# Attention with linear features: queries' and keys' projections in own pairs of PSUM banks, one lasting pair for all transposes, and a new order of a step

## The chip, the cores and the metric

The kernel runs on one core of a Trainium2 chip. Time is device microseconds (us) of one execution. Engines: PE is TensorE, which multiplies and transposes and writes to PSUM; DVE (VectorE) and ACT (ScalarE) read PSUM and work elementwise; POOL is GpSimd; SP issues most transfers. PSUM has eight banks; a tile of 2 x 512 float32 per partition is a pair of them. Each engine takes its own instructions in order and waits on semaphores for the others.

## The reference, cut to what matters

```
# 8 batches x 8 heads, 576 positions, head_dim 64, 128 features
def phi(x):
    proj = x @ w_phi
    proj = proj - max(abs(proj), axis=-1)
    return concat([exp(proj), exp(-proj)], axis=-1)
q_p, k_p = phi(q), phi(k)
kv  = sum over positions of k_p (x) v        # per batch and head
z   = sum over positions of k_p
out = (q_p @ kv) / (q_p @ z + 1e-6)
# then  h = x @ w_in;  x = (h * cos(h)) @ w_out     (4608 tokens, 512 -> 2048 -> 512)
# then  8 experts, one per token: gate * relu(x @ w1[e]) @ w2[e]
```

## The kernel before

Attention comes first, the dense layer and the experts follow. Attention works on 16 items; an item is two batches times two heads. Turned, an item has nine blocks of 128 columns (each for two heads' halves); they are cut into five groups, `GR=[(0,2),(2,2),(4,1),(5,2),(7,2)]`: four full ones of two blocks and a half one in the middle. The first item runs in `begin(m)`, the others in `step(j,m)`, m from 0 to 4, one group a step. A step is a software pipeline. For item j and step m it does:

- turn: transposes raw q or k of item j+1 (tile pt) and ACT copies them to qT or kT
- outT: transposes finished rows xs of item j-1, two steps old, to po, and ACT copies them to xo
- proj: PE multiplies qT and kT of group m with w_phi into pj; DVE takes the largest absolute value (m_q, m_k) and subtracts it (t_q, t_k), four instructions
- kexp: ACT makes ke = exp of plus and minus t_k of the group before
- qexp: PE transposes t_q of two groups before (ptt), ACT makes qx = exp of plus and minus it
- kv: PE multiplies ke with v; kvfin copies the sum (kvz) by ACT after groups 2 and 4; in step 0 of an item, kv has 24 matmuls instead of 16, in step 4 it has 8
- num: PE multiplies qx of item j-1 with kvz into pn; DVE makes rd, its reciprocal and xs, which I call the trio

The order on an engine is that of the code, since each instruction is put through `keep`. Among these instructions lie those of the dense layer's weights, one piece a step: ACT's d_t and w, DVE's L457 to L460 (two, one, one, none, in turn).

PSUM in the steps: pj one pair, tr one pair (shared in turn by pt and ptt), po one pair, kv and pn one bank each. In pj the queries lie in columns 0 to 255 of both banks and the keys in 256 to 511. Tiles on one bank are guarded as a whole: an engine that wants a bank waits for the other engines' accesses to it.

Of the kernel before, what the change touches and what calls it, by code (L numbers as in the profile page):

```python
# [45 lines left out]
def attention(tc, ctx, S, ident, q, k, v, w_phi, xt):  # L46
# [73 lines left out]

    T={}
    H=64
    def to(tag,name):

        if not pairs: return ps.tile([P,512],F32,tag=dict(tr="tr",po="nm")[tag],name=name)
        return pairs[0].tile([P,2,512],F32,tag=tag,name=name)
    def over(dst,c,src):

        if not pairs: keep(nc.tensor.transpose(dst[:,c*P:(c+1)*P],src,ident)); return
        for r in range(2): keep(nc.tensor.transpose(dst[:,r,c*H:(c+1)*H],src[r*H:(r+1)*H],ident[r*H:(r+1)*H,r*H:(r+1)*H]))  # L130
    def got(dst,a,c):
        return dst[:,a*P:c*P] if not pairs else dst[:,:,a*H:c*H].rearrange("p r (c t) -> p c r t",t=H)
    def like(x): return x if not pairs else x.rearrange("p (c r t) -> p c r t",r=2,t=H)
    def turn(i,m,tag="tr"):
        pt=to(tag,f"pt_{i}_{m}")
        c=0; made=[]
        for t,c0,n in TURN[m]:
            if (t,i) not in T: T[t,i]=S("xT",f"{t}T_{i}")
            a=c
            for b in range(c0,c0+n):  # L140
                over(pt,c,block(raws[t,i],b)); c+=1
            made.append((like(T[t,i][:,c0*P:(c0+n)*P]),got(pt,a,c)))
        def vec():
            for x,p in made: keep(nc.scalar.copy(x,p))
        return vec

    ts={}
    pj=pp.tile([P,2,512],F32,name="pj")
    def proj(i,g):
        c0,n=GR[g]  # L150
        vecs=[]
        other=i==0 and g in (1,4)
        out=[ps.tile([P,512],F32,tag="nm",name=f"pj_{i}_{g}_{s}") for s in range(2)] if other else [pj[:,s,:] for s in range(2)]
        for t,o in (("q",0),("k",256)):
            x=T[t,i]
            for c in range(n):
                for s in range(2):
                    keep(nc.tensor.matmul(out[s][:,o+c*F:o+(c+1)*F],x[s*D:(s+1)*D,(c0+c)*P:(c0+c+1)*P],w2[s*D:(s+1)*D,:],start=True,stop=True))  # L158
            tt=ts[t,i,g]=S(t+"t",f"t_{t}_{i}_{g}")
            def vec(t=t,o=o,tt=tt):  # L160
                gg=pj[:,:,o:o+n*F].rearrange("p s (c f) -> p s c f",f=F)
                m=ap.tile([P,4],F32,tag=t+"m",name=f"m_{t}_{i}_{g}")[:,:2*n].rearrange("p (s c) -> p s c",s=2)
                keep(nc.vector.tensor_reduce(m,gg,AX.X,ALU.max,apply_absolute_value=True))  # L163
                keep(nc.vector.tensor_tensor(tt[:,:n*256].rearrange("p (s c f) -> p s c f",s=2,f=F),gg,  # L164
                    m.unsqueeze(3).to_broadcast([P,2,n,F]),ALU.subtract))
            vecs.append(vec)
        def by_bank():
            ms=[]
            for s in range(2):
                ms.append(ap.tile([P,4],F32,tag="qk"[s]+"m",name=f"m_{s}_{i}_{g}"))  # L170
                nc.vector.tensor_reduce(ms[s],out[s].rearrange("p (c f) -> p c f",f=F),AX.X,ALU.max,apply_absolute_value=True)
            for o,t in ((0,"q"),(1,"k")):
                for s in range(2):
                    nc.vector.tensor_tensor(ts[t,i,g][:,s*256:(s+1)*256].rearrange("p (c f) -> p c f",f=F),out[s][:,o*256:(o+1)*256].rearrange("p (c f) -> p c f",f=F),
                        ms[s][:,2*o:2*o+2].unsqueeze(2).to_broadcast([P,2,F]),ALU.subtract)
        return [by_bank] if other else vecs
# [37 lines left out]
    def qexp(i,g):  # L214

        n=GR[g][1]; tt=ts.pop(("q",i,g))
        pt=to("tr",f"ptt_{i}_{g}")
        for c in range(n):
            for s in range(2): over(pt,2*c+s,tt[:,(s*n+c)*F:(s*n+c+1)*F])
        w=n*P  # L220
        x=ap.tile([P,1024],F32,tag="qx",name=f"qx_{i}_{g}",bufs=4)
        qx[i,g]=x[:,:4*w].rearrange("p (k h c) -> p k h c",h=2,k=2)
        made=[(like(x[:,kk*2*w:(kk+1)*2*w]),got(pt,0,2*n)) for kk in range(2)]
        def vec():
            for (o,p),sign in zip(made,(1.0,-1.0)): keep(nc.scalar.activation(o,p,AF.Exp,scale=sign))
        return vec

    xss={}; xos={}
    def num(i,g):
# [18 lines left out]
        return vec  # L248

    def outT(i,g):  # L250

        t0,n=GR[g]
        if g==0: xos[i]=ap.tile([P,9*P],F32,tag="xo",name=f"xo_{i}")
        xo=xos[i]; xs=xss.pop((i,g))
        po=to("po",f"po_{i}_{g}")
        for t in range(n): over(po,t,xs[:,t*P:(t+1)*P])
        def vec():
            keep(nc.scalar.copy(like(xo[:,t0*P:(t0+n)*P]),got(po,0,n)))
            if g==4:
# [4 lines left out]
    FIRST=((),((0,1),),((0,2),(0,4)),((1,0),(1,1)),((1,2),(1,3)))
    def at(j,m): return divmod(5*j+m,5)
# [4 lines left out]
        if m==2: ld("v",j+1)  # L270
    def begin(m):

        vecs=[turn(i,n) for i,n in FIRST[m]]
        if m>1: vecs+=[lambda: kexp(0,m-2),qexp(0,m-2)]
        for f in vecs: f()
        loads(0,m)
        yield
# [4 lines left out]
        if m==4: kvfin(0,0)
        yield
    def step(j,m):

# [20 lines left out]
        yield
# [812 lines left out]
```

## Time and profile before

| | |
|---|---|
| three runs | 1597.93, 1592.8, 1597.95 us, median 1597.93 |
| the profiled execution | 1593.69 us, its span 1592.0 us |
| PE busy | 1551.5 us, 97% of the span |
| DVE busy | 1116.7 us, 70% |
| ACT busy | 879.0 us, 55% |
| POOL busy | 398.3 us, 25% |

The shares are means over stages of different kinds. Attention's matmuls run up to 344 us, where the dense layer's have begun; the experts' begin at 1132 us. A matmul's end in the records is modelled, so starts are compared with starts. Records of PE count two for each float32 matmul of projections, kv and pn, and one for each transpose.

### The profile page before, as it was taken

How to read it: one execution, taken by the hardware profiler on the slowest of the kernel's cores; microseconds unless marked ns; L12 is line 12 of the kernel's file. 1: busy time of each engine (PE TensorE's matmuls, PEld its weight loads, DVE VectorE, ACT ScalarE, POOL GpSimd, SP SyncE). 2: the span in 40 equal slices, each digit the busy share in tenths (PEclk: the TensorE clock that was granted, in tenths of full speed). 3: DMA queues.
4: the chain of work that ended last, by engine and by line, in shares of the span. 5: the costliest groups of instructions: out<-in, count | busy, mean ns of one | idle time of the engine just before them, and what ended most of it. 6: DMA issues, size and time to landing. Idle time of an engine off the chain costs nothing.

```text
span 1592.0 us, 35511 instructions
## 1 busy us (share of the span) xinstructions
PE 1551.5 (97%) x14065; PEld 1338.9 (84%) x14065; DVE 1116.7 (70%) x2305; ACT 879.0 (55%) x1627; POOL 398.3 (25%) x356
## 2 busy tenths in 40 slices
PE   8899998989999999999999999999999999999998
PEld 7788888878888888888888888888898899899986
DVE  6998988978666767675766667655775656666646
ACT  6777777766534444343534344444765656565646
POOL 1101101120233333243333433333212112212212
PEclk9999999999999999999999999999999999999999
DMA  7755555313200101010100001004749667766752
GB/s 213 213 157 161 153 156 161 105 65 125 92 29 9 40 14 40 7 41 14 40 14 30 24 7 41 7 1 159 237 154 319 224 221 276 239 222 220 246 196 86
DMA packets 140851, 189.33 MB, mean 119 GB/s; under 512 B 63015, under 2 KB 87719, under 8 KB 140674
## 3 DMA queue, kind: packets, MB, share of 16 engines
q1 hardware_dynamic: 132754, 166.11, 33.4%
q0 software_dynamic: 7760, 20.79, 3.9%
q8 instruction: 112, 1.84, 0.5%
q14 instruction: 65, 0.53, 0.1%
q10 hardware_dynamic: 160, 0.07, 0.0%
HBM read 155.88 MB, written 31.82 MB: 118 GB/s over the span
## 4 chain that ended last, share of the span: by engine, by line
PE 81%; DVE 11%; DMA 3%; ACT 2%; issue 2%; POOL 0%; POOLq 0%; DVEq 0%; SPq 0%; ACTq 0%
PE ph L514 24%; PE acc L554 19%; PE mh L822 12%; PE po L834 12%; PE acc L559 5%; DMA out_dram<-o,mrec 3%; PE pj L158 3%; DVE t_k L164 2%; DVE t_q L164 2%; DVE m_q L163 2%; DVE m_k L163 2%; PE kv L204 2%; PE pn L240 2%; PE px L804 1%; DVE xs L247 1%
## 5 line engine op out<-in xcount | busy, mean ns | idle before, releaser
L514 PE MATMUL ph<-x,w 128*128 128x512 f32 x1728 | 418.3, 391 | 1.9 <-DVE fr L536 1.9
L514 PEld LDWEIGHTS ph<-x,w 128*128 128x128 f32 x1728 | 322.6, 188 | 70.0 <-DVE fr L536 2.5
L543 POOL TENSOR_TENSOR gl<-fr,gh 128x512 fp32r<-128x512 f32 x130 | 195.5, 1506 | 432.8 <-DVE gh L542 387.3
L777 DVE TENSOR_TENSOR m<-raw,m 128x512 fp32r<-128x512 f32 x320 | 208.3, 688 | 100.7 <-ACT m L776 72.7
L554 PE MATMUL acc<-w,gh 128*128 128x512 f32 x896 | 275.8, 389 | 0.0
L527 ACT ACTIVATE n<-ph 128x512 int32<-128x512 f32 x144 | 86.0, 597 | 271.3 <-PE ph L514 270.8
L776 ACT CAST m<-raw 128x512 fp32r<-128x512 f32 x320 | 188.0, 619 | 39.2 <-PE mh L822 31.0
L822 PE MATMUL mh<-xT,m 128*128 128x256 f32 x1728 | 201.1, 277 | 0.0
L822 PEld LDWEIGHTS mh<-xT,m 128*128 128x128 f32 x1728 | 197.8, 188 | 1.1 <-DVE hl L825 0.8
L529 DVE SCALAR_TENSOR_TENSOR fr<-ph,n 128x512 f32<-128x512 f32 x144 | 99.2, 689 | 140.5 <-ACT n L527 125.6
L554 PEld LDWEIGHTS acc<-w,gh 128*128 128x128 f32 x896 | 168.2, 188 | 35.0
L590 DVE SCALAR_TENSOR_TENSOR junk<-x1T,wg 128x512 f32<-128x512 f32 x224 | 181.0, 808 | 0.0
L834 PE MATMUL po<-m,hh 128*128 128x512 f32 x576 | 179.6, 393 | 0.0
L554 PE MATMUL acc<-w,gl 128*128 128x512 f32 x448 | 174.3, 389 | 0.0
L532 ACT ACTIVATE fr<-fr 128x512 f32<-128x512 f32 x144 | 91.1, 632 | 117.9 <-DVE fr L529 117.8
L536 DVE SCALAR_TENSOR_TENSOR fr<-fr,ph 128x512 f32<-128x512 f32 x144 | 98.8, 686 | 78.2 <-ACT fr L534 78.1
L834 PEld LDWEIGHTS po<-m,hh 128*128 128x128 f32 x576 | 105.2, 188 | 19.7
L834 PE MATMUL po<-m,hl 128*128 128x512 f32 x288 | 112.4, 390 | 0.0
L883 POOL DMA_INDIRECT out_dram<-o,mrec x38 | 42.7, 1124 | 265.5 <-ACT o L882 251.3
L554 PEld LDWEIGHTS acc<-w,gl 128*128 128x128 f32 x448 | 84.1, 188 | 17.5
L534 ACT ACTIVATE fr<-fr 128x512 f32<-128x512 f32 x143 | 90.4, 632 | 4.3
L240 PE MATMUL pn<-kvz,qx 128*64 128x65 f32 x2304 | 86.9, 226 | 3.0 <-DVE xs L247 1.7
(228 smaller groups left out, 2256.6 us busy)
## 6 DMA issues: line engine op xcount, KB each, us to landing
raw<-in_moe_w_dram SPq DMA_DIRECT2D x160, 512.0 KB
xt<-xo SPq DMA_DIRECT2D x16, 576.0 KB
xr<-xt SPq DMA_DIRECT2D x36, 256.0 KB
raw_q<-in_q_dram SPq DMA_DIRECT2D x32, 256.0 KB
raw_k<-in_k_dram SPq DMA_DIRECT2D x32, 256.0 KB
st<-in_moe_w_in_dram SPq DMA_DIRECT2D x16, 512.0 KB
st<-in_moe_w_out_dram SPq DMA_DIRECT2D x16, 512.0 KB
v<-in_v_dram SPq DMA_DIRECT2D x62, 128.0 KB
```

What stands on the lines that cost most here:

```text
L240: keep(nc.tensor.matmul(o[64*c:64*c+64],x[:,sg,h,t*P+64*c:t*P+64*c+64],kvs[i,bb][:,2*h+sg,:],start=sg==0,stop=sg==1,skip_group_check=True))
L514: nc.tensor.matmul(ph,A[:,ws],xhl[u,d][k],start=n[0]==0,stop=n[0]==11); n[0]+=1
L529: ins=nc.vector.scalar_tensor_tensor(g,ph,INV2PI,n,op0=ALU.mult,op1=ALU.subtract)
L532: nc.scalar.activation(g,g,AF.Sin,scale=math.pi)
L536: out0[0]=nc.vector.scalar_tensor_tensor(g,g,-0.5,ph,op0=ALU.add,op1=ALU.mult)
L543: nc.gpsimd.tensor_tensor(gl,g,f32(gh),ALU.subtract)
L554: nc.tensor.matmul(accs[u][c],A[:,ws],B,start=(f==0 and k==0),stop=(f==NF-1 and k==2))
L590: return lambda: tc.keep_in_program_order(nc.vector.scalar_tensor_tensor(junk,x1T[u,c],1.0,wg[e],op0=ALU.mult,op1=ALU.mult,accum_out=lgs[u ...
L776: keep(nc.scalar.copy(h,a))
L777: keep(nc.vector.tensor_tensor(l,a,f32(h),ALU.subtract))
L822: nc.tensor.matmul(ph[:,f2*T:(f2+1)*T],A[:,ws],B[d//2][:,xs],start=n==0,stop=n==11); n+=1
L834: nc.tensor.matmul(po[c],A[:,ws],B,start=(f==0 and j==0),stop=(f==NF2-1 and j==2))
```

## The change

The queries' projection keeps pj; the keys' gets a pair of its own, pjk. There is one pair tr from the first instruction to the end of attention for all transposes of raw data (columns of chunks 0 to 3) and of t_q (chunks 4 to 7); in the first item its two banks are used in turn as whole banks. po has no tile any more: the turned outputs are written into pjk, beside the keys (from chunk 4 on). In the first item the groups alternate between pj and pjk. The order within a step is new. The number of instructions of each kind is the same.

```diff
     pk=ctx.enter_context(tc.tile_pool(name="a_kv",bufs=1,space=PSUM,side="right"))
-    first=ExitStack()
-    ps=first.enter_context(tc.tile_pool(name="a_first",bufs=2,space=PSUM,side="right"))
-    pairs=[]
+    pj,pjk=(pp.tile([P,2,512],F32,tag=n,name=n) for n in ("pj","pjk"))
+    tr=pk.tile([P,2,512],F32,tag="tr",name="tr")
+    flat=itertools.count()
...
-    def to(tag,name):
-
-        if not pairs: return ps.tile([P,512],F32,tag=dict(tr="tr",po="nm")[tag],name=name)
...
-    def got(dst,a,c):
-        return dst[:,a*P:c*P] if not pairs else dst[:,:,a*H:c*H].rearrange("p r (c t) -> p c r t",t=H)
...
+    def whole(srcs):
+
+        pt=tr[:,next(flat)%2,:]
+        for c,x in enumerate(srcs): keep(nc.tensor.transpose(pt[:,c*P:(c+1)*P],x,ident))
+        return pt
+    def turn(i,m,pt=None,base=0):
...
+        if pt is None:
+            pt=whole(srcs)
+            def vec():
+                for x,a,b in made: keep(nc.scalar.copy(x,pt[:,a*P:b*P]))
+        else:
+            for c,x in enumerate(srcs): over(pt,base+c,x)
+            def vec():
+                for x,a,b in made: keep(nc.scalar.copy(like(x),got(pt,base+a,base+b)))
+        return vec
...
+    def proj(i,g,t,out,o=0):
+        c0,n=GR[g]
+        x=T[t,i]
...
+                keep(nc.tensor.matmul(out[:,s,o+c*F:o+(c+1)*F],x[s*D:(s+1)*D,(c0+c)*P:(c0+c+1)*P],w2[s*D:(s+1)*D,:],start=True,stop=True))
+        tt=ts[t,i,g]=S(t+"t",f"t_{t}_{i}_{g}")
         def vec():
-            for x,p in made: keep(nc.scalar.copy(x,p))
+            gg=out[:,:,o:o+n*F].rearrange("p s (c f) -> p s c f",f=F)
+            m=ap.tile([P,4],F32,tag=t+"m",name=f"m_{t}_{i}_{g}")[:,:2*n].rearrange("p (s c) -> p s c",s=2)
+            keep(nc.vector.tensor_reduce(m,gg,AX.X,ALU.max,apply_absolute_value=True))
+            keep(nc.vector.tensor_tensor(tt[:,:n*256].rearrange("p (s c f) -> p s c f",s=2,f=F),gg,
+                m.unsqueeze(3).to_broadcast([P,2,n,F]),ALU.subtract))
...
-    pj=pp.tile([P,2,512],F32,name="pj")
-    def proj(i,g):
...
-        vecs=[]
-        other=i==0 and g in (1,4)
-        out=[ps.tile([P,512],F32,tag="nm",name=f"pj_{i}_{g}_{s}") for s in range(2)] if other else [pj[:,s,:] for s in range(2)]
-        for t,o in (("q",0),("k",256)):
...
     def qexp(i,g):
 
         n=GR[g][1]; tt=ts.pop(("q",i,g))
-        pt=to("tr",f"ptt_{i}_{g}")
...
-        w=n*P
+        srcs=[tt[:,(s*n+c)*F:(s*n+c+1)*F] for c in range(n) for s in range(2)]
...
+        if i==0 and g<3:
+            pt=whole(srcs)
+            made=[(x[:,kk*w:(kk+1)*w],pt[:,:w]) for kk in range(2)]
+        else:
+            for c,y in enumerate(srcs): over(tr,4+c,y)
+            made=[(like(x[:,kk*w:(kk+1)*w]),got(tr,4,4+2*n)) for kk in range(2)]
...
-        po=to("po",f"po_{i}_{g}")
-        for t in range(n): over(po,t,xs[:,t*P:(t+1)*P])
+        po,base=(pjk,4) if (i,g)<(NI-1,0) else (tr,2*(g%2))
+        for t in range(n): over(po,base+t,xs[:,t*P:(t+1)*P])
         def vec():
-            keep(nc.scalar.copy(like(xo[:,t0*P:(t0+n)*P]),got(po,0,n)))
+            keep(nc.scalar.copy(like(xo[:,t0*P:(t0+n)*P]),got(po,base,base+n)))
...
-        vecs=proj(0,m)
+        if m==4: vecs=[proj(0,m,"q",pj),proj(0,m,"k",pjk)]
+        else:
+            out=(pj,pjk)[m%2]
+            vecs=[proj(0,m,"q",out),proj(0,m,"k",out,256)]
+            if m==1: vecs=[lambda: by_bank(0,m,out)]
...
     def step(j,m):
 
-        vecs=[]
-        if j==1 and m==0: vecs=[turn(1,4),turn(2,0,"po")]
-        elif j+1<NI: vecs=[turn(j+1,m)]
-        i,g=at(j-1,m-2)
-        if i>=0: vecs.append(outT(i,g))
-        for f in vecs: f()
-        if (j,m)==(1,0): kexp(0,3)
-        i,g=at(j,m-1)
-        if i<NI: kexp(i,g)
+        vecs=[]; dve=[]
+        i,g=at(j,m-2); oi,og=at(j-1,m-2); ki,kg=at(j,m-1)
+        if j<NI: dve.append(proj(j,m,"q",pj))
+        if oi>=0: vecs.append(outT(oi,og))
+        if j<NI: dve.append(proj(j,m,"k",pjk))
+        two=j==1 and m==0
+        if two: vecs+=[lambda: kexp(0,3),turn(2,0,pjk,4)]
+        if i<NI: last=qexp(i,g)
+        if two: vecs.append(turn(1,4,tr))
+        elif j+1<NI: vecs.append(turn(j+1,m,tr))
+        if i<NI: vecs.append(last)
+        for f in vecs+dve: f()
         loads(j,m)
-        vecs=proj(j,m) if j<NI else []
-        i,g=at(j,m-2)
-        if i<NI: qexp(i,g)()
         yield
-        vecs.append(num(j-1,m))
         if i<NI: kv(i,g)
-        for f in vecs: f()
+        last=num(j-1,m)
         if i<NI and g in (2,4): kvfin(i,g//4)
+        if ki<NI: kexp(ki,kg)
+        last()
...
-    first.close()
-    pairs.append(ctx.enter_context(tc.tile_pool(name="a_pairs",bufs=1,space=PSUM,side="right")))
```

PE, the instructions of one whole step (item 3, step 3); raw_q and qT are the raw and turned queries, xs the finished rows. Before:

```order
L130 MATMUL pt_3_1649<-ident,raw_q_1015 128x64 x8
L130 MATMUL po_1_1658<-ident,xs_1_1531 128x64 x4
L158 MATMUL pj<-w_90,qT_1098 128x128 x4
L158 MATMUL pj<-w_90,kT_883 128x128 x4
L130 MATMUL ptt_1_1678<-ident,t_q_1_1496 128x64 x8
L240 MATMUL pn_3_1690<-kvz_1_1558,qx_3_1400 64x65 x16
L204 MATMUL kv_0_1620<-v_1113,ke_1_1579 64x65 x16
```

The same step in the change:

```order
L156 MATMUL pj<-w_90,qT_1072 128x128 x4
L125 MATMUL pjk<-ident,xs_1_1492 128x64 x4
L156 MATMUL pjk<-w_90,kT_868 128x128 x4
L125 MATMUL tr<-ident,t_q_1_1409 128x64 x8
L125 MATMUL tr<-ident,raw_q_997 128x64 x8
L201 MATMUL kv_0_1552<-v_1088,ke_1_1579 64x65 x16
L240 MATMUL pn_3_1645<-kvz_1_1493,qx_3_1323 64x65 x16
```

The projections moved to the front with the outputs' transposes between them, the raw transposes went behind those of t_q, and pn went from before kv to the end.

DVE, one step (item 4, step 0), with the engines whose semaphores it waits on. Before:

```order
L163 TENSOR_REDUCE m_q_0_1897<-pj 128x4 [waits PE_49]
L164 TENSOR_TENSOR t_q_0_1836<-pj,m_q_0_1897 128x512 [waits DVE_49]
L163 TENSOR_REDUCE m_k_0_1900<-pj 128x4
L164 TENSOR_TENSOR t_k_0_1841<-pj,m_k_0_1900 128x512 [waits DVE_49,Activation_49]
L245 TENSOR_SCALAR rd_0_1903<-pn_0_1854 128x4 [waits PE_49]
```

In the change:

```order
L161 TENSOR_REDUCE m_q_0_1781<-pj 128x4 [waits PE_49]
L162 TENSOR_TENSOR t_q_0_1749<-pj,m_q_0_1781 128x512 [waits DVE_49]
L161 TENSOR_REDUCE m_k_0_1784<-pjk 128x4 [waits Activation_49]
L162 TENSOR_TENSOR t_k_0_1758<-pjk,m_k_0_1784 128x512 [waits DVE_49]
L245 TENSOR_SCALAR rd_0_1833<-pn_0_1812 128x4 [waits PE_49]
```

The order is the same; m_k waits for ACT now, whose copy xo reads the same pair.

ACT, around the end of item 4's last step and the next step's beginning. Before:

```order
L211 COPY kvz_0_2257<-kv_0_2069 128x260
L461 CAST w_0_1810<-d_t_0_1809 128x512
L144 COPY kT_2264<-pt_0_2263 128x512
L258 COPY xo_2019<-po_3_2273 128x256
L184 ACTIVATE ke_4_2280<-t_k_4_2212 128x4x128 x2
L225 ACTIVATE qx_3_2302<-ptt_3_2293 128x512 x2
```

In the change:

```order
L208 COPY kvz_0_2168<-kv_0_1986 128x260
L181 ACTIVATE ke_3_2170<-t_k_3_2034 128x4x128 x2
L464 CAST w_0_1743<-d_t_0_1742 128x512
L258 COPY xo_1943<-pjk 128x256
L147 COPY kT_2204<-tr 128x512
L225 ACTIVATE qx_3_2195<-tr 128x512 x2
```

The copy xo stands first in a step, and the two instructions of ke moved from the middle of a step to its end.

## Rows read from the trace of the kernel before

**Rows 1.** Windows: stretch, its length, each engine's busy us, granted clock, DMA share, GB/s.
```profile
20.00:40.00 20.00, 17.41 (x416) 16.37 (x414) 15.11 (x34) 14.09 (x31) 0.54 (x3) 0.91 0.75 193
80.00:120.00 40.00, 36.33 (x924) 33.73 (x924) 36.21 (x82) 30.29 (x70) 3.68 (x9) 1.00 0.54 156
600.00:1100.00 500.00, 500.00 (x2291) 412.43 (x2290) 334.32 (x749) 206.53 (x327) 184.00 (x129) 1.00 0.11 32
```

**Rows 2.** Chain of waits, 200 to 300 us, its shares by line.
```profile
by line: PE pj L158 15.9%; DVE t_q L164 11.6%; DVE m_q L163 11.2%; DVE t_k L164 11.1%; DVE m_k L163 9.6%; PE kv L204 8.0%; PE pn L240 7.4%; DVE xs L247 3.7%; issue 3.7%; PE pt L130 2.8%; PE ptt L130 1.9%; DVE d_t L460 1.8%; DVE d_t L458 1.7
```

**Rows 3.** Waits of PE, 80 to 320 us: total us, times, longest.
```profile
PE pj L158 <- DVE t_k L164: 12.5, 29, 0.7
PE ptt L130 <- ACT qT L144: 4.3, 4, 1.2
```

**Rows 4.** Waits of DVE, 80 to 320 us: the same columns.
```profile
DVE m_q L163 <- PE pj L158: 11.2, 19, 0.7
```

**Rows 5.** Lines of DVE, 80 to 320 us: count | busy us, mean ns | idle before.
```profile
L163 DVE TENSOR_REDUCE m_q<-pj 128x4 f32<-128x512 f32 (+1 forms) x61 | 38.9, 638 | 12.2 <-PE pj L158 11.2
...
L460 DVE SCALAR_TENSOR_TENSOR d_t<-st,d_t 128x512 int32<-128x512 int32 x16 | 10.9, 682 | 0.0
```

**Rows 6.** Timeline of PE: start, duration, line, output<-inputs, matmuls, idle before and releaser.
```profile
228.61 1.57 PE L204 MATMUL kv<-v,ke 128*64 128x65 f32 x48
230.11 0.46 PE L130 MATMUL pt<-ident,raw_k 64*128 64x64 f32 x8
230.41 0.29 PE L130 MATMUL po<-ident,xs 64*128 64x64 f32 x4
230.53 0.66 PE L158 MATMUL pj<-w,qT 64*128 64x128 f32 x8
231.03 0.61 PE L158 MATMUL pj<-w,kT 64*128 64x128 f32 x8
231.48 0.41 PE L130 MATMUL ptt<-ident,t_q 64*128 64x64 f32 x8
231.82 1.16 PE L240 MATMUL pn<-kvz,qx 128*64 128x65 f32 x32
232.80 1.10 PE L204 MATMUL kv<-v,ke 128*64 128x65 f32 x32
233.84 0.28 PE L130 MATMUL pt<-ident,rl_k 64*128 64x64 f32 x2
...
250.49 0.46 PE L130 MATMUL pt<-ident,raw_k 64*128 64x64 f32 x8
```

**Rows 7.** Timeline of DVE, 250 to 255 us.
```profile
250.60 0.15 DVE L245 TENSOR_SCALAR rd<-pn 128x4 f32<-128x4 f32 x1
...
251.34 0.68 DVE L460 SCALAR_TENSOR_TENSOR d_t<-st,d_t 128x512 int32<-128x512 int32 x1
252.08 0.69 DVE L163 TENSOR_REDUCE m_q<-pj 128x4 f32<-128x512 f32 x1
...
253.41 0.68 DVE L163 TENSOR_REDUCE m_k<-pj 128x4 f32<-128x512 f32 x1
...
254.80 0.15 DVE L245 TENSOR_SCALAR rd<-pn 128x4 f32<-128x4 f32 x1
```

**Rows 8.** Timeline of ACT, 250 to 255 us.
```profile
251.00 0.59 ACT L144 COPY kT<-pt 128x512 f32<-128x512 f32 x1 [1.16 <-PE pt L130]
251.48 0.38 ACT L258 COPY xo<-po 128x256 f32<-128x256 f32 x1
251.74 1.16 ACT L184 ACTIVATE ke<-t_k 128x512 f32<-128x512 f32 x2
252.79 1.08 ACT L225 ACTIVATE qx<-ptt 128x512 f32<-128x512 f32 x2
```

**Rows 9.** Timeline, all engines, around the second item's first step.
```profile
22.96 0.46 PE L130 MATMUL pt<-ident,raw_q 64*128 64x64 f32 x8 [2.29 <-DVE t_k L174]
...
25.00 2.00 PE L240 MATMUL pn<-kvz,qx 128*64 128x65 f32 x32
```

More of the change, by code (lines that the diff above doesn't have):

```diff
@@ L122, in attention @@
     H=64
-    def to(tag,name):
-        if not pairs: return ps.tile([P,512],F32,tag=dict(tr="tr",po="nm")[tag],name=name)
-        return pairs[0].tile([P,2,512],F32,tag=tag,name=name)
     def over(dst,c,src):
-        if not pairs: keep(nc.tensor.transpose(dst[:,c*P:(c+1)*P],src,ident)); return
         for r in range(2): keep(nc.tensor.transpose(dst[:,r,c*H:(c+1)*H],src[r*H:(r+1)*H],ident[r*H:(r+1)*H,r*H:(r+1)*H]))
-    def got(dst,a,c):
-        return dst[:,a*P:c*P] if not pairs else dst[:,:,a*H:c*H].rearrange("p r (c t) -> p c r t",t=H)
@@ L133, in like, with got @@
[L133 to L136, printed above, removed]
+    def got(dst,a,c): return dst[:,:,a*H:c*H].rearrange("p r (c t) -> p c r t",t=H)
+    def like(x): return x.rearrange("p (c r t) -> p c r t",r=2,t=H)
+    def whole(srcs):
[3 more added lines that the diff above has]
+    def turn(i,m,pt=None,base=0):
+        c=0; made=[]; srcs=[]
@@ L137, in turn @@
         for t,c0,n in TURN[m]:
             if (t,i) not in T: T[t,i]=S("xT",f"{t}T_{i}")
[L139 to L143, printed above, removed]
-            for x,p in made: keep(nc.scalar.copy(x,p))
+            srcs+=[block(raws[t,i],b) for b in range(c0,c0+n)]
+            made.append((T[t,i][:,c0*P:(c0+n)*P],c,c+n)); c+=n
+        if pt is None:
[6 more added lines that the diff above has]
+                for x,a,b in made: keep(nc.scalar.copy(like(x),got(pt,base+a,base+b)))
@@ L145, in turn @@
         return vec
     ts={}
-    pj=pp.tile([P,2,512],F32,name="pj")
-    def proj(i,g):
+    def proj(i,g,t,out,o=0):
         c0,n=GR[g]
-        vecs=[]
-        other=i==0 and g in (1,4)
-        out=[ps.tile([P,512],F32,tag="nm",name=f"pj_{i}_{g}_{s}") for s in range(2)] if other else [pj[:,s,:] for s in range(2)]
-        for t,o in (("q",0),("k",256)):
[L155 to L168, printed above, removed]
-            for s in range(2):
[L170 to L176, printed above, removed]
@@ new lines, in proj, with vec @@
+        x=T[t,i]
+        for c in range(n):
+            for s in range(2):
+                keep(nc.tensor.matmul(out[:,s,o+c*F:o+(c+1)*F],x[s*D:(s+1)*D,(c0+c)*P:(c0+c+1)*P],w2[s*D:(s+1)*D,:],start=True,stop=True))
+        tt=ts[t,i,g]=S(t+"t",f"t_{t}_{i}_{g}")
+        def vec():
+            gg=out[:,:,o:o+n*F].rearrange("p s (c f) -> p s c f",f=F)
[3 more added lines that the diff above has]
+                m.unsqueeze(3).to_broadcast([P,2,n,F]),ALU.subtract))
@@ new lines, in proj, with by_bank @@
+        return vec
+    def by_bank(i,g,out):
+        ms=[]
+        for s in range(2):
+            ms.append(ap.tile([P,4],F32,tag="qk"[s]+"m",name=f"m_{s}_{i}_{g}"))
+            keep(nc.vector.tensor_reduce(ms[s],out[:,s,:].rearrange("p (c f) -> p c f",f=F),AX.X,ALU.max,apply_absolute_value=True))
+        for o,t in ((0,"q"),(1,"k")):
+            for s in range(2):
+                keep(nc.vector.tensor_tensor(ts[t,i,g][:,s*256:(s+1)*256].rearrange("p (c f) -> p c f",f=F),out[:,s,o*256:(o+1)*256].rearrange("p (c f) -> p c f",f=F),
+                    ms[s][:,2*o:2*o+2].unsqueeze(2).to_broadcast([P,2,F]),ALU.subtract))
@@ L216, in qexp @@
         n=GR[g][1]; tt=ts.pop(("q",i,g))
-        pt=to("tr",f"ptt_{i}_{g}")
-        for c in range(n):
-            for s in range(2): over(pt,2*c+s,tt[:,(s*n+c)*F:(s*n+c+1)*F])
-        w=n*P
+        srcs=[tt[:,(s*n+c)*F:(s*n+c+1)*F] for c in range(n) for s in range(2)]
+        w=2*n*P
         x=ap.tile([P,1024],F32,tag="qx",name=f"qx_{i}_{g}",bufs=4)
-        qx[i,g]=x[:,:4*w].rearrange("p (k h c) -> p k h c",h=2,k=2)
-        made=[(like(x[:,kk*2*w:(kk+1)*2*w]),got(pt,0,2*n)) for kk in range(2)]
+        qx[i,g]=x[:,:2*w].rearrange("p (k h c) -> p k h c",h=2,k=2)
+        if i==0 and g<3:
[4 more added lines that the diff above has]
+            made=[(like(x[:,kk*w:(kk+1)*w]),got(tr,4,4+2*n)) for kk in range(2)]
         def vec():
@@ L271, in begin @@
     def begin(m):
-        vecs=[turn(i,n) for i,n in FIRST[m]]
-        if m>1: vecs+=[lambda: kexp(0,m-2),qexp(0,m-2)]
-        for f in vecs: f()
+        for i,n in FIRST[m]: turn(i,n)()
+        if m>1:
+            kexp(0,m-2); qexp(0,m-2)()
         loads(0,m)
         yield
-        vecs=proj(0,m)
+        if m==4: vecs=[proj(0,m,"q",pj),proj(0,m,"k",pjk)]
[3 more added lines that the diff above has]
+            if m==1: vecs=[lambda: by_bank(0,m,out)]
         if m<1: warm(3)
@@ L284, in step @@
     def step(j,m):
-        vecs=[]
-        if j==1 and m==0: vecs=[turn(1,4),turn(2,0,"po")]
-        elif j+1<NI: vecs=[turn(j+1,m)]
-        i,g=at(j-1,m-2)
-        if i>=0: vecs.append(outT(i,g))
-        for f in vecs: f()
-        if (j,m)==(1,0): kexp(0,3)
-        i,g=at(j,m-1)
-        if i<NI: kexp(i,g)
+        vecs=[]; dve=[]
[10 more added lines that the diff above has]
+        for f in vecs+dve: f()
         loads(j,m)
-        vecs=proj(j,m) if j<NI else []
-        i,g=at(j,m-2)
-        if i<NI: qexp(i,g)()
         yield
-        vecs.append(num(j-1,m))
         if i<NI: kv(i,g)
-        for f in vecs: f()
+        last=num(j-1,m)
         if i<NI and g in (2,4): kvfin(i,g//4)
+        if ki<NI: kexp(ki,kg)
+        last()
         if j==NI-1 and m==4: pctx.close()
```

## Prediction

> **What bounds the kernel now.** I read the windows by stage first. In the dense layer (600 to 1100 us is a stretch of it) PE is busy 500.0 of 500 us; the change touches nothing there. In the attention stage PE and DVE are both busy about 36 of 40 us and neither is full [rows 1]. So two engines share the limit there, and the 4 us that each lacks must be a mutual wait. The chain of waits between 200 and 300 us says the same: it alternates between the projection's matmuls (pj, 15.9%) and the four DVE instructions on each group, about 10 to 12% each [rows 2]. The table of waits from 80 to 320 us gives sizes. PE's projections waited 12.5 us for t_k, and PE's transposes of t_q waited 4.3 us for ACT's copy out of the one tr tile [rows 3]; DVE's m_q waited 11.2 us for the projections [rows 4]. ACT is busy 30 of 40 us and seldom waited for. DMA is at half its capacity.
>
> That is a ping-pong over one pair of banks: PE fills pj with queries and keys, stands still for all four DVE instructions, then DVE stands still while PE refills. The list of DVE instructions holds 60 to 61 groups in 240 us, so 12 items at 20.0 us each [rows 5]. Without its 0.93 us of waiting per item (11.2 / 12) DVE would need 19.1 us. PE waited 16.8 us in the two large rows of its table, so PE alone would need 18.6 at most. DVE is the tighter engine, and 0.93 us per item, or 14 us over 15 items, is what can be had from it at most.
>
> **The change, step by step.** I take a step as PE issues it [rows 6]. Start to start: eight transposes of raw data 0.30 us, po 0.12, queries' projection 0.50, keys' projection 0.45, transposes of t_q 0.34, pn 0.98, kv of 16 matmuls 1.04; together 3.73 (230.11 to 233.84). The long kv of the first step of an item takes 1.50 instead of 1.04. DVE [rows 7]: the trio rd, reciprocal, xs takes 0.74 (250.60 to 251.34), the four instructions on a group 2.72 (252.08 to 254.80), of which the queries' half is 1.33. In three steps of four (by the code's order) a piece of the weights' decode follows the trio; L460's takes 0.68, and the two others are as long or longer [rows 5].
>
> *Removed: the shared pair.* The next queries' projection now needs only t_q, and DVE's m_q needs only that projection, which PE issues while DVE is still at m_k and t_k. The 11.2 us of DVE's wait on projections goes: minus 0.93 us an item. The 12.5 us on PE's side are the other face of it and are not counted again. A single tr now holds both kinds of transposes and is refilled once a step, after ACT has had some 2 us for it, so the 4.3 us go as well; they are PE's, which is not the tighter engine, and bring nothing by themselves.
>
> *Moved: pn goes to the end of PE's step.* This is the new wait. Before, pn was complete long before DVE came to rd. Now rd, reciprocal and xs wait for the last matmul of the step, with the next group's four DVE instructions queued behind them. Let T be the end of a t_k. From T PE must still do po, keys, t_q's transposes, raw transposes, kv, pn: 0.12 + 0.45 + 0.34 + 0.30 + 1.04 + 0.98 = 3.23 us. I add 0.1 for the change of tile form below, 0.06 for the start, and 0.2 for the way from the last matmul to the reader (raw transposes start at 250.49, take 0.30, and their reader starts at 251.00 after waiting [rows 6, 8]). So pn is readable at T + 3.59. DVE comes to rd at T + 0.74 + 2.72 = T + 3.46, plus its decode piece. The wait is 0.13 us in a step without a decode piece and nothing in the three others. With the long kv it is 0.59. In the step with a half group I count half groups at half on PE and at 0.6 on DVE (the mean 638 ns over four full and one half gives 0.43 against 0.69) [rows 5, 7]: PE 2.73 against DVE 2.39, 0.34; in the one after it 0.27; in the last, with a half kv, nothing. Since only one step in four is without a decode piece, this is (0.13 + 0.59 + 0.34 + 0.27) / 4 = 0.33 us an item.
>
> *Added: the turned outputs lie in pjk beside the keys, so m_k waits for ACT's copy xo.* Nothing on the rows of before shows this wait; its two ends are nothing and a full miss. The copy can start when the keys' projection is done, T + 0.06 + 0.57 + 0.2, and takes 0.38 [rows 8]: T + 1.2. DVE comes to m_k at T + 0.74 + 1.33 = T + 2.07 at the earliest. It is covered by 0.9 us, if ACT is free. ACT's work in a full step is turn 0.48, xo 0.26, ke 1.05, qx 1.08 start to start [rows 8], 2.9 us, and with a decode piece of the shape of turn, 0.59, some 3.5, in a step of 3.9. I take nothing, and keep the miss as a rival.
>
> *Added: one more change of tile form per PE step* (64x128 to 64x64 and back around po). Rows: t_q's eight transposes take 0.34 before pn, another form, and the raw eight 0.30 before po, the same form: 0.04. kv takes 1.04 before a new form and pn 0.98 before the same: 0.06 [rows 6]. I take 0.1 a step. The Trainium skill (TensorEngine Tiling (Array Packing), Key Properties) says that a change of tiling mode drains the engine; no row here shows a full drain at such a place. By the 0.2 us from a last matmul to its reader as the price of a drain, an estimate, the waits on pn would grow by 0.1 us each and the sum by 1.5 us; by the rows it stays as above.
>
> *The start.* PE stands 2.29 us before the first step of the second item, waiting for all of DVE's work on the last early group, and the clock then falls: 32 matmuls of pn take 2.00 us at 25 us against 1.16 later, and the granted clock of the window is 0.91 [rows 1, 6, 9]. With own pairs the queries' projection starts after half of that DVE work, so the wait splits in two. Between nothing and 2.5 us (1 of waiting, 0.84 of pn and as much of kv); I take 1.5. Loads, decode pieces and DMA issues keep their steps. On SP's queue the store of a finished item, which waits for ACT, now stands ahead of the next load of raw_k; that load is for an item that is turned a whole item of 20 us later, which covers it.
>
> **Sum.** Per item 0.93 - 0.33 = 0.60 us; 15 items, 9.0 us; with the start 10.5; I take off 0.5 for semaphores, which makes 10. The profiled execution took 1593.7 us, so 1583.7. The runs shown are 1592.8, 1597.9 and 1597.95, 2.5 us higher in the mean than the profiled one; on their scale I say 1586, or 0.6% less than the mean.
>
> **Rivals.**
> 1. *DVE never waits.* If PE's step is a little shorter than its parts, the 0.33 vanish, the small idle pieces go too, and the start gives 2.5: about 1.1 us an item, 19 us, 1577 on the scale of the runs. For it: PE's demand of 18.6 us is under DVE's 19.1. Against it: pn stands last, with no slack in a long kv step.
> 2. *Nothing comes out.* PE's step needs 0.3 us more than the rows say, through semaphores on kv and pn or through forms. Then the wait on pn reaches the steps with decode pieces too: 0.73 us an item plus what is handed on, some 0.9, which eats the 0.93. 1594 to 1596. For it: the two engines' steps are within 0.2 us of each other.
> 3. *Slower: ACT comes late with xo.* DVE waits at m_k, in order, with the rest of its work behind. It decides from the point where xo ends later than 2.07 us after T; that needs ACT to be 0.9 us behind in a plain step, and 0.2 to 0.3 in one with kvz and two decode pieces. 0.25 us in each of 75 steps costs 19 us: 1605. For it: ACT now has kexp at the end of its step, directly ahead of the next xo, and 3.5 us of work in 3.9. Against it: 2.07 us of DVE work cover it.
>
> **How the numbers follow.** The forecast 0.47 (1580 to 1592), DVE full 0.20, nothing 0.20, slower 0.13. One measurement of this kernel tells about 0.5%, 8 us, from no change. The forecast's own range lies mostly under 1590: 0.37 of it faster, 0.10 the same. So faster 0.57, same 0.30, slower 0.13. The range leaves out the outer half of rivals 1 and 3: 1574 to 1602.
>
> **What would show it.** DVE's wait of m_q on projections must be nearly gone from the table of waits, and a wait of rd on pn of some 4 us over twelve items must stand in its place, above all after long kv. PE's wait for t_k should now stand at the keys' projection or at po. m_k must show no wait on xo; if it shows several us, rival 3 holds. An item should take 19.4 us. The gap of 2.29 us at 22.96 should be shorter, and the clock near it higher. The prediction is wrong if an item takes 20 us or more, or if the waits go and the items do not get shorter, which would mean that instructions themselves got longer.

## The result and the profile after

The changed kernel took 1583.09 us in the median of 4 runs (1582.37 to 1583.64) beside 1596.78 for the kernel before (4 runs, 1592.8 to 1597.95); the ratio is 0.9918 with a 95% interval of 0.9899 to 0.9937. The profiled execution took 1583.64 us against 1593.69, 10.05 us less. So it is faster, by 0.6% between the profiled executions and 0.8% between the runs. The medians of the runs lie 13.7 us apart, more than the two profiled executions: of the kernel before, the profiled execution was one of the quicker ones.

Windows of the changed kernel, the columns as in [rows 1]:

```profile
20.00:40.00 20.00, 17.65 (x427) 16.15 (x426) 16.24 (x35) 15.17 (x36) 0.54 (x3) 1.00 0.76 203
80.00:120.00 40.00, 38.27 (x987) 36.13 (x986) 37.34 (x85) 33.02 (x76) 4.93 (x9) 1.00 0.54 157
600.00:1100.00 500.00, 500.00 (x2305) 412.60 (x2304) 331.49 (x739) 205.11 (x325) 183.84 (x131) 1.00 0.12 33
```

In the attention stage both limiting engines are fuller: PE 38.3 of 40 us, DVE 37.3. The dense stretch is untouched. The granted clock at 20 to 40 us is 1.00 instead of 0.91. The waits of 80 to 320 us, which answer [rows 3, 4]:

```profile
PE pjk L125 <- DVE rd L245: 9.7, 17, 1.6
PE tr L125 <- issue: 1.1, 1, 1.1
...
DVE rd L245 <- PE pn L240: 8.5, 16, 1.9
DVE x L506 <- ACT x L505: 0.4, 1, 0.4
```

m_q's wait on the projections has gone from DVE's table, and so has PE's wait of t_q's transposes for ACT. In their place rd waits for pn. PE stands ahead of po, which overwrites the pair that t_k reads. The table names rd, the instruction behind t_k, but po is released as t_k ends: in PE's timeline the queries' projection starts at 238.12 and po only at 239.54, and t_k runs from 238.70 to 239.39.

The length of an item is best taken from the copies kvz, two in an item. In the kernel before, the first copy of the fourth item and that of the fifteenth on ACT:

```profile
85.91 0.38 ACT L211 COPY kvz<-kv 128x260 f32<-128x260 f32 x1 [0.33 <-PE kv L204]
...
305.68 0.38 ACT L211 COPY kvz<-kv 128x260 f32<-128x260 f32 x1 [0.22 <-PE kv L204]
```

In the changed kernel:

```profile
84.54 0.40 ACT L208 COPY kvz<-kv 128x260 f32<-128x260 f32 x1
...
294.78 0.40 ACT L208 COPY kvz<-kv 128x260 f32<-128x260 f32 x1
```

Eleven items are 219.77 and 210.24 us, 19.98 and 19.11 an item. DVE's lines over exactly these stretches show what the 0.87 us are made of. The kernel before:

```profile
L164 DVE TENSOR_TENSOR t_k<-pj,m_k 128x512 f32<-128x512 f32 (+1 forms) x56 | 35.8, 640 | 5.6
...
L164 DVE TENSOR_TENSOR t_q<-pj,m_q 128x512 f32<-128x512 f32 (+1 forms) x55 | 35.1, 638 | 1.9
L163 DVE TENSOR_REDUCE m_q<-pj 128x4 f32<-128x512 f32 (+1 forms) x55 | 35.0, 637 | 10.6 <-PE pj L158 9.6
```

The changed kernel:

```profile
L162 DVE TENSOR_TENSOR t_k<-pjk,m_k 128x512 f32<-128x512 f32 (+1 forms) x55 | 35.1, 638 | 1.9
L161 DVE TENSOR_REDUCE m_q<-pj 128x4 f32<-128x512 f32 (+1 forms) x55 | 34.6, 629 | 0.0
...
L245 DVE TENSOR_SCALAR rd<-pn 128x4 f32<-128x4 f32 (+1 forms) x55 | 8.5, 154 | 6.5 <-PE pn L240 6.3
```

The last column is the idle time ahead of the instruction. Per item: m_q 10.6 / 11 = 0.96 us gone, rd 6.5 / 11 = 0.59 new, and ahead of t_k 3.7 / 11 = 0.34 gone, in a gap that carries no releaser and that no table of waits lists. Together that is 0.71. The 0.16 that is left of the 0.87 lies in the busy time of the windows of the two stretches (DVE's is the third of the engines), 197.40 and 195.69 us. The lines themselves add up to nearly the same in both, so most of it is overlap: an instruction that follows directly starts before the end shown for the one ahead, and an instruction that waited does not.

```profile
85.91:305.68 219.77, 201.50 (x5130) 187.41 (x5130) 197.40 (x444) 170.89 (x394) 25.16 (x48) 1.00 0.54 156
```
```profile
84.54:294.78 210.24, 200.43 (x5134) 188.57 (x5131) 195.69 (x444) 172.61 (x394) 25.07 (x48) 1.00 0.57 161
```

The start did not gain, it lost. The first kvz comes at 24.06 us instead of 20.72; by the second one the two kernels are nearly level (32.87 and 32.52). PE of the changed kernel there:

```profile
10.51 0.66 PE L131 MATMUL tr<-ident,raw_q 128*128 128x128 f32 x4 [0.52 <-ACT qT L143]
11.84 0.65 PE L131 MATMUL tr<-ident,t_q 128*128 128x128 f32 x4 [0.68 <-ACT qT L143]
...
15.48 0.65 PE L131 MATMUL tr<-ident,raw_k 128*128 128x128 f32 x4 [0.68 <-ACT kT L143]
16.81 0.66 PE L131 MATMUL tr<-ident,t_q 128*128 128x128 f32 x4 [0.68 <-ACT kT L143]
...
24.47 0.71 PE L156 MATMUL pj<-w,qT 64*128 64x128 f32 x8 [0.46 <-DVE t_q L162]
25.86 0.71 PE L156 MATMUL pjk<-w,kT 64*128 64x128 f32 x8 [0.68 <-DVE t_k L162]
...
28.70 1.10 PE L240 MATMUL pn<-kvz,qx 128*64 128x65 f32 x32
```

The gap of 2.29 us [rows 9] has become 0.46 and 0.68, as foretold, and pn takes 1.10 instead of 2.00. But six times before, PE waits 0.52 to 0.68 us, 3.8 in all, for ACT's copy of the transposes just ahead. Those went into the other bank of the pair. But the pair is one tile, and the next writer is made to wait for the last reader of the whole tile; the experiment with two tiles bears this out.

### The profile page after: what moved, and what is told of

It is laid out like the page before. It is cut to its first block, busy times and chain, and to the rows that moved or that the text cites. A ratio compares the mean times of both kernels' runs of the same rounds, so it can differ in the third digit from the quotient of the medians.

```text
span 1581.9 us, 35508 instructions
## 1 busy us (share of the span) xinstructions
PE 1550.4 (98%) x14065; PEld 1339.4 (85%) x14065; DVE 1113.6 (70%) x2303; ACT 880.6 (56%) x1627; POOL 397.0 (25%) x356
## 4 chain that ended last, share of the span: by engine, by line
PE 82%; DVE 12%; DMA 4%; issue 2%; ACT 0%; SPq 0%; POOLq 0%; DVEq 0%
PE ph L517 25%; PE acc L557 19%; PE mh L825 12%; PE po L837 11%; PE acc L562 6%; DMA xg<-x1d,mrec 2%; PE kv L201 2%; DVE t_q L162 2%; DVE t_k L162 2%; DVE m_q L161 2%; DVE m_k L161 2%; PE pn L240 2%; DVE xs L247 1%; PE pjk L156 1%; PE px L807 1%
## 5 line engine op out<-in xcount | busy, mean ns | idle before, releaser
L201 PE MATMUL kv<-v,ke 128*64 128x65 f32 x2560 | 93.3, 225 | 0.9 <-issue 0.9
```

The lines of the kernel that those rows point to most:

```text
L201: keep(nc.tensor.matmul(o[f0:f0+64],e[:,col+f0:col+f0+64],vh[:,h,9 if cc==4 and bb else cc,:],start=start,stop=cc==(4,8)[bb],skip_group_ch ...
```

## The experiments

Each ratio is to the kernel before, timed again beside each of three groups of experiments. The medians of the kernel before were 1595.76, 1596.87 and 1595.88 us there, so a difference of medians across groups, or from the changed kernel's 1583.09, is good to about 1 us.

**Sharing a pair again.** All else is as changed; the keys' projection goes beside the queries'.

```
-        if j<NI: dve.append(proj(j,m,"k",pjk))
+        if j<NI: dve.append(proj(j,m,"k",pj,256))
```

> The changed kernel with the keys' projection put back beside the queries' in one pair of banks (the other pair holds only the turned outputs); order and all else as changed. Theory A: the separation is what brings the gain. Then m_q waits for the projections again, about 0.7 us a step less what the wait on pn gives back; an item takes 19.9 to 20.2 us and the time is 1593 to 1598. Rival B: the new order or the lasting pair of transposes brings most of it: an item stays under 19.5 us, 1583 to 1588.

1596.18 us, ratio to before 1.0005 (0.9996 to 1.0013): the whole gain is gone. An item takes 20.09 us (86.27 to 307.26). DVE's waits of this kernel, 80 to 320 us:

```profile
DVE m_q L161 <- PE pj L156: 7.8, 20, 0.7
DVE rd L245 <- PE pn L240: 2.3, 14, 0.2
```

The wait of m_q is back. Theory A holds: without own banks the new order, the lasting pair and the start come to nothing together. One more thing went back with it: the idle time ahead of t_k is 5.9 us over its eleven items. The next experiments take that apart.

**The gap ahead of t_k.** In the program of the kernel before, 71 of the 78 t_k wait for two semaphores (two groups of the first item are done bank by bank and are not counted): DVE's for m_k, and ACT's for the last reader of the tile that is overwritten. In the changed kernel m_k waits for ACT anyway, because xo reads its pair; that wait covers the older reader too, and all but two t_k have only DVE's left. So I gave m_k that wait in the kernel before and in the one with the shared pair (`kx` holds the second exponential of each group's keys):

```
 ins=keep(nc.vector.tensor_reduce(m,gg,AX.X,ALU.max,...))
+if t=="k" and 5*i+g-3 in kx:
+    tc.add_manual_dep(ins.ins,kx[5*i+g-3].ins.name,
+        mybir.DependencyInfo(mybir.DependencyClass.Sync,...))
```

> The kernel before, with one edit: m_k, which has no semaphore to wait for there, is told to wait for ACT's last reader of the tile that t_k will overwrite (three groups back, long done), so that t_k has one semaphore to wait for (DVE's, for m_k) instead of two. Theory A: in the kernel before each t_k started 0.10 us after the end of m_k and in the changed one 0.034 us, because an instruction with two semaphores to wait for starts later, although both are long set. Then the idle time ahead of t_k falls from 5.6 to 1.9 us over eleven items, and some 70 times 0.067 us, 4.7 us, come off the kernel before: 0.3%. Rival B: the 0.10 us come from m_k and t_k reading the same banks that PE filled together; then the gap stays, or it moves ahead of m_k, and the time does not change.

1592.11 us, ratio 0.9979 (0.9969 to 0.9990). DVE of this kernel:

```profile
251.63 0.68 DVE L163 TENSOR_REDUCE m_k<-pj 128x4 f32<-128x512 f32 x1
252.34 0.69 DVE L166 TENSOR_TENSOR t_k<-pj,m_k 128x512 f32<-128x512 f32 x1
```

From start to start it is 0.71 us. In the kernel before it was 0.79: m_k at 253.41 [rows 7], with the same 0.68 us, and

```profile
254.20 0.69 DVE L164 TENSOR_TENSOR t_k<-pj,m_k 128x512 f32<-128x512 f32 x1
```

The idle time ahead of t_k is 1.9 us over eleven items, as theory A has it, and it did not move ahead of m_k: m_k starts 0.61 us after t_q's start with this wait (251.02 and 251.63) and without it (252.80 and 253.41 in the kernel before). The idle time ahead of m_q grew from 10.6 to 11.8 us, so PE takes a part back. The time gives 3.8 us for the 4.7 expected.

> The same edit on the kernel of the third experiment (the changed kernel with queries and keys in one pair of banks, 1596.2 us). Theory A: t_k's gap falls from 5.9 to 1.9 us over eleven items and 4 to 6 us come off: 1590 to 1592; what then still lies between it and the changed kernel, 7 to 9 us, is the wait of m_q on the shared pair. Rival B: PE and DVE wait for each other over the shared pair, so a shorter DVE list only lengthens m_q's wait: 1595 to 1596.

1592.59 us, ratio 0.9980 (0.9971 to 0.9988), 3.6 us under the kernel with the shared pair (4.0 by the ratios): theory A, at the lower edge of its range of 4 to 6. What then lies between it and the changed kernel, 9.5 us, goes with the shared pair itself.

**pn ahead of kv.** The changed kernel, with the order of these two as it was:

```
-        if i<NI: kv(i,g)
         last=num(j-1,m)
+        if i<NI: kv(i,g)
```

> The changed kernel with one edit: in each step PE issues pn ahead of kv again, so that pn ends about 1 us earlier. Theory A: the wait of rd on pn (8.5 us over 12.5 items, 0.68 an item) is what keeps DVE from being full; it goes, an item falls from 19.2 to about 18.6 us, and some 9 us come off: 1574. Rival B: PE, with 18.5 us of work an item, is as tight; its own waits shrink but the item only falls by 0.2 us: 1580. Rival C: the wait moves to the queries' projection, which now follows kv, and nothing comes off: 1583.

1579.82 us, ratio 0.9898 (0.9883 to 0.9913), 3.3 us under the changed kernel; an item takes 18.68 us (85.87 to 291.37). The expected 0.6 us of an item became 0.43, between A and B; the time is rival B's 1580. The wait on pn is gone, and a smaller one has come. DVE's waits, 80 to 320 us:

```profile
DVE m_k L161 <- ACT xo L258: 2.1, 6, 0.5
DVE rd L245 <- PE pn L240: 0.9, 2, 0.7
```

With kv last, ACT stands at the copy kvz until kv ends (11.6 us in its table), and comes late to xo: the mechanism of my third rival, in an order that I had not weighed it for. The profiled execution also started 2.3 us late (last section), so its time and its items don't match one to one.

**Tile forms.** Each block of po ahead of one half of the keys' projection, in three steps of five:

```
         for c in range(n):
+            if between: between(c)
             for s in range(2):
```

> The changed kernel, but in the steps whose outputs and keys both have two blocks (three steps of five from the second item on, some 43 steps) the two blocks of po are issued one ahead of each half of the keys' projection, which adds two changes of tile form to such a step and no work: some 86 changes more. Theory A: a change costs some 0.03 to 0.05 us, PE gets 3 to 4 us more and the time rises by 0 to 4 us: 1583 to 1587. Rival B: each change drains the engine, 0.2 us: 17 us more of PE, 1592 to 1600.

1585.58 us, ratio 0.9933 (0.9919 to 0.9946): 2.5 us for some 86 changes, 0.03 us each; an item went from 19.11 to 19.38 us, 0.045 for each of its six. PE's timeline shows it directly: po and the keys together take 0.66 us from start to start (245.55 to 246.21) instead of 0.61 in the changed kernel (243.83 to 244.44). At 0.2 us each, PE would have had 1.2 us more work an item. Its waits at po could have hidden a part of that, but they did not shrink (9.6 us, 17 times, from 80 to 320 us, beside 9.7). So that price is excluded here.

**xo late.** ACT copies the raw transposes ahead of xo:

```
-        if oi>=0: vecs.append(outT(oi,og))
+        xo=outT(oi,og) if oi>=0 else None
 ...
+        if xo: vecs.append(xo)
         if i<NI: vecs.append(last)
```

> The changed kernel, but on ACT the copy xo comes behind the copy of the raw transposes instead of ahead of it, which ends xo about 1.1 us later (some 2.3 us after the end of the previous t_k instead of 1.2). The prediction held that m_k needs it by 2.07 us in a step without decode work and by 1.6 in a half step. Theory A: then m_k waits 0.2 to 0.3 us in these steps, some 1.3 full and one half step an item, a part of it in place of the wait on pn: 3 to 8 us more, 1586 to 1591. Rival B: xo has more slack than that (ACT runs ahead, or the wait on pn gives it back): no change, 1583.

1587.45 us (1585.41 to 1589.92), ratio 0.9938 (0.9924 to 0.9953); its interval still touches that of the changed kernel, but all six runs lie above all four of it, and the median lies in theory A's range. Its waits, 80 to 320 us:

```profile
DVE m_k L161 <- ACT xo L258: 5.7, 14, 0.5
DVE rd L245 <- PE pn L240: 2.0, 5, 1.2
```

Now m_k waits 0.4 us, 14 times, and rd waits 6.5 us less than in the changed kernel: the new wait mostly takes the old one's place. An item takes 19.18 us (88.44 to 299.47), 0.07 more. One case, in the same timelines: t_k ends at 209.21 (T), xo ends at 211.84, T + 2.63, and m_k starts at 211.87, 0.48 us after it could have. So m_k needed xo by T + 2.18, near the 2.07 of the prediction, but the price in the rival was too high. The 4.4 us between the medians (3.2 by the ratios) are not explained by items: fifteen times 0.07 is 1. The profiled execution had a late start of 2.3 and lost another 1.6 by the fourth item's kvz; why, and whether the other runs did, is open.

**Two tiles at the start.** The first item's whole transposes go into two one-bank tiles, as before the change:

```
-        pt=tr[:,next(flat)%2,:]
+        pt=two.tile([P,512],F32,tag="tr",name=f"tr_{next(flat)}")
```

> The changed kernel, but in the first item the whole transposes go into two separate tiles of one bank each, taken in turn, as the kernel before had it; the lasting pair is made afterwards. Theory A: the start of the changed kernel lost time because PE's transposes wait for ACT's copy out of the other half of the same tile (six waits of 0.52 to 0.68 us, 3.8 us, between 10 and 22 us). Then these waits go, the first kvz copy comes at about 21 us instead of 24.1, and 2 to 3.3 us come off: 1580 to 1581. Rival B: the waits only fill time that DVE's work needs anyway; the first step of the second item starts where it does now, and the time stays at 1583.

1580.74 us, ratio 0.9907 (0.9893 to 0.9922), 2.3 us under the changed kernel. Its copies kvz (count: shortest, median, longest ns; first and last start):

```profile
L210 ACT COPY kvz<-kv x32: 376/394/396, 21.0 to 319.0; 128x260 f32<-128x260 f32 x32
```

In the changed kernel they run from 24.1 to 321.9: the 3 us are won at the first item and kept to the last. Theory A. The intervals of the two kernels overlap, so it is the trace that decides: of the six waits only one of 0.24 us is left, and a seventh in the changed kernel, 0.68 us ahead of PE's first projection (6.13) for ACT's copy qT, is gone too.

**Together.** The last three build on each other: both gains, then ACT's exponentials of the keys ahead of kvz, then on PE the transposes of t_q and of raw data ahead of po and the keys, which wait for t_k:

```
-        if i<NI and g in (2,4): kvfin(i,g//4)
         if ki<NI: kexp(ki,kg)
+        if i<NI and g in (2,4): kvfin(i,g//4)
```

```
-        if oi>=0: vecs.append(outT(oi,og))
-        if j<NI: dve.append(proj(j,m,"k",pjk))
+        def keys():
+            if oi>=0: vecs.append(outT(oi,og))
+            if j<NI: dve.append(proj(j,m,"k",pjk))
 ...
+        if not start:
+            late=vecs; vecs=[]
+            keys(); vecs+=late
```

> The changed kernel with both edits of the first two experiments: two tiles for the whole transposes of the first item, and pn ahead of kv in each step. Theory A: the two gains lie in different stretches (before 25 us, and in the fifteen items behind) and add: 1583.1 - 2.3 - 3.3 = 1577.5, an item 18.7 us, first kvz at 21. Rival B: the items run into a common bound (loads or ACT) and the start's 3 us come back as a wait: 1579 to 1580.

1576.16 us, ratio 0.9876 (0.9858 to 0.9895): the gains add (1577.5 expected).

> As the one before, and ACT makes the exponentials of the keys ahead of the copy kvz instead of behind it. Theory A: with pn first, kv ends PE's step, so ACT stands at kvz for kv (11.6 us over 12.5 items) and comes late to the next xo; m_k waited 2.1 us and po 2.1 us for that. With the exponentials ahead of kvz both go, an item falls by 0.2 to 0.3 us and 2 to 4 us come off: 1574 to 1575. Rival B: the waits of m_k only take what PE would have made DVE wait anyway; no more than 1 us comes off.

1576.13 us, ratio 0.9870 (0.9852 to 0.9888): no change, rival B. The 2.1 us of m_k are gone, so it was ACT's standing at kvz that made xo late, and DVE waits 1.2 us at m_q and 1.2 at rd.

> As the kernel with all three edits, and in each step PE's transposes of t_q and of the raw data come ahead of po and the keys' projection, which have to wait for t_k; so PE has work while it waits. Theory A: PE's remaining wait at po (4.9 us over 11 items with pn ahead of kv) goes, pn and the keys come earlier after t_k, and up to 3 us come off the kernel with three edits. Rival B: with three edits DVE has next to no wait left but the small gaps ahead of each instruction, so PE's waits are free and nothing changes (within 1 us).

1575.10 us (1572.87 to 1578.70), ratio 0.9872 (0.9852 to 0.9891); 1.0 us under the one before it, which these runs can't tell from nothing: rival B, as far as the time goes. In the profiled execution, the quickest of the four, an item takes 18.30 us (83.20 to 284.54) against 18.59. DVE of this kernel over these eleven items, and their window:

```profile
L164 DVE TENSOR_TENSOR t_k<-pjk,m_k 128x512 f32<-128x512 f32 (+1 forms) x55 | 35.1, 638 | 1.9
L163 DVE TENSOR_REDUCE m_q<-pj 128x4 f32<-128x512 f32 (+1 forms) x55 | 34.6, 630 | 0.0
...
L248 DVE TENSOR_SCALAR rd<-pn 128x4 f32<-128x4 f32 (+1 forms) x55 | 8.3, 151 | 0.0
```
```profile
83.20:284.54 201.34, 198.76 (x5132) 185.90 (x5128) 193.24 (x441) 168.11 (x394) 25.17 (x48) 1.00 0.59 170
```

DVE has only the gaps of 0.034 us ahead of instructions that wait for their neighbour; PE is busy 198.8 of 201.3 us. This version beats both kernels: all its runs are under all of the changed kernel's.

## Why the prediction was right

The mechanism was foretold: the wait on the shared pair goes, a smaller one on pn comes, and an item gets shorter (19.4 us foretold, 19.11 measured). That the size came out so closely is partly luck. 10 us less was foretold for the profiled execution, and 10.05 came, but on the scale of the runs 1586 was foretold, and 1583.1 came. And by the steps, terms were off in opposite directions: the items brought 13.1 us instead of 9.0, the start lost 1.2 instead of bringing 1.5, and 1.9 went at the end of the stage, where 0.5 were taken off for semaphores.

- **Removed: the shared pair.** 0.93 us an item was foretold, 0.96 measured, and the shared pair put back takes the gain away. The step that I did not have: since xo reads the keys' pair, m_k now carries the wait for ACT, and t_k has one semaphore instead of two, worth 0.34 us an item as idle time. This part does not need the separation (with the shared pair it brought 3.6 us). Neither the waits nor the releasers showed it, only the last column of DVE's lines and the semaphores listed for t_k in the section on the change.
- **Moved: pn to the end.** The mechanism and the place were right, the size was not: 0.59 us an item instead of 0.33. DVE of the changed kernel after a long kv, first t_k, then the next group's t_k and rd:

```profile
219.49 0.69 DVE L162 TENSOR_TENSOR t_k<-pjk,m_k 128x512 f32<-128x512 f32 x1
...
222.87 0.69 DVE L162 TENSOR_TENSOR t_k<-pjk,m_k 128x512 f32<-128x512 f32 x1
224.18 0.16 DVE L245 TENSOR_SCALAR rd<-pn 128x4 f32<-128x4 f32 x1 [0.62 <-PE pn L240]
```

  T is 220.18, and rd starts at T + 4.00; 3.59 and the 0.46 of the longer kv make 4.05. The next t_k ends at T + 3.38 instead of 3.46, since t_k has become quicker; so the wait is 0.62 instead of 0.59. The other kinds of steps show 0.19 to 0.41, once 0.99, where 0.13 to 0.34 were foretold. And there are 14 waits in eleven items, where the sum counts one an item.
- **Added: m_k behind xo.** A cost of nothing was foretold, and m_k stands in no table of waits of 80 to 320 us. In a step of the changed kernel t_k ends at 208.83 and xo runs from 209.95 to 210.32, T + 1.49 where T + 1.2 was worked out; the cover is 0.6 us rather than 0.9, and in the experiment with xo late (T + 2.63) it is used up.
- **Added: a change of tile form.** 0.1 us a step was taken. PE of the changed kernel, from one queries' projection to the next:

```profile
243.28 0.72 PE L156 MATMUL pj<-w,qT 64*128 64x128 f32 x8
243.83 0.28 PE L125 MATMUL pjk<-ident,xs 64*128 64x64 f32 x4
243.94 0.67 PE L156 MATMUL pjk<-w,kT 64*128 64x128 f32 x8
...
246.02 1.10 PE L240 MATMUL pn<-kvz,qx 128*64 128x65 f32 x32
247.05 0.49 PE L156 MATMUL pj<-w,qT 64*128 64x128 f32 x4
```

  That is 3.77 us against 3.73 [rows 6], and the test with more changes gives 0.03 to 0.045 each. The Trainium skill (TensorEngine Tiling (Array Packing), Key Properties) says that a change of tiling mode drains the engine and gives no price. The prediction's 1.5 us put the price at 0.2 us, an estimate of its own; the runs don't agree with that price here.
- **The start.** A gain of 1.5 us was taken; it lost. At the fourth item's kvz the changed kernel is 1.37 us ahead, and three items at 0.87 would make 2.6, so the start cost 1.2. With two tiles the lead there is 4.70 (81.21 against 85.91), a gain of 2.1. So the split of the wait, with the clock, brought what was foretold and a little more, and the step that failed is one that I did not cost: that whole transposes into the two banks of one tile no longer overlap with ACT's copies.
- **Sum.** Fifteen items at 0.87 are 13.1 us, less 1.2 for the start: 11.9, which is the lead at the last kvz (321.94 against 333.87). The remaining 1.9 are given back where PE goes over to the dense layer (ph). The kernel before:

```profile
330.35 1.10 PE L204 MATMUL kv<-v,ke 128*64 128x65 f32 x32
331.39 3.02 PE L514 MATMUL ph<-x,w 128*128 128x512 f32 x12
```

  The changed kernel:

```profile
318.12 1.41 PE L201 MATMUL kv<-v,ke 128*64 128x65 f32 x32
319.37 1.11 PE L240 MATMUL pn<-kvz,qx 128*64 128x65 f32 x32
321.13 3.06 PE L517 MATMUL ph<-x,w 128*128 128x512 f32 x12 [0.66 <-ACT xo L258]
```

  The last kv leads by 12.23 us, ph by 10.26. pn, which stood ahead of this kv, now stands behind it (1.10), and PE then waits 0.66 for the copy xo; kv itself took 0.21 longer. So the order with pn last costs once more at the end of the stage, a step that the prediction did not have.
- **Rivals.** DVE never waits: not in this order, but the last kernel of the experiments, with pn ahead of kv, nearly reaches it at 18.30 us an item. Nothing comes out: excluded. Slower by xo: excluded here, and cheaper than thought.

## What to carry to other kernels

When two engines hand one buffer to and fro, ask what a buffer for each half would bring: here it took away about the whole wait. But look at what becomes last in the step: what DVE needed first (pn) had been put behind what no engine was waiting for (kv), and turning that round gave 3 us more. Read the idle column of every line over whole periods, also where no releaser is named: small equal gaps, seventy to the stage, were worth 3.8 us. A tile that spans two banks was one tile to the dependency tracking, so alternating its halves was no double buffer.

## What the hardware showed that I had not expected

In these traces t_k with two semaphores to wait for starts some 0.07 us later than with a single one, even when the second was set long before: t_k starts 0.79 us after m_k's start with two and 0.71 with one, within the same kernel too. In the changed kernel's first item, where t_k still waits for two:

```profile
19.94 0.68 DVE L161 TENSOR_REDUCE m_k<-pjk 128x4 f32<-128x512 f32 x1
20.73 0.69 DVE L162 TENSOR_TENSOR t_k<-pjk,m_k 128x512 f32<-128x512 f32 x1
...
27.48 0.69 DVE L161 TENSOR_REDUCE m_k<-pjk 128x4 f32<-128x512 f32 x1 [0.35 <-ACT kT L147]
28.20 0.69 DVE L162 TENSOR_TENSOR t_k<-pjk,m_k 128x512 f32<-128x512 f32 x1
```

The second pair, with one, has 0.72 beside 0.79. In the program the second wait is an instruction of its own (EventSemaphore) ahead of t_k: 71 times in the kernel before, twice in the changed one, so the two do not quite have the same number of instructions of each kind. That the 0.07 us are its time is likely, but no trace shows it. A single wait cost m_k nothing (0.61 us from t_q's start with it and without).

PE's first matmuls run at half their later pace, and for how long differs between executions. With pn ahead of kv the profiled one shows, up to about 10 us:

```profile
4.90 1.06 PE L131 MATMUL tr<-ident,raw_k 128*128 128x128 f32 x4
...
8.65 1.46 PE L317 MATMUL warm<-zt 128*128 128x512 bf16 x3
```

The changed kernel's execution has 0.60 and 0.82 for the same two, although the code is the same there and the granted clock reads 1.00 in both. The first kvz then comes at 26.39 instead of 24.06 us, and the same happened with the late xo (26.35). Differences of 2 us between single executions of this kernel can be that alone.
